# Planned order of an attention and MoE kernel: finer fillers, quartered transposes, ScalarE as a third copier

## The chip, the core and the metric

The kernel runs on one core of one Trainium2 chip. The time is device microseconds of one launch, from the first instruction to the last with what the device adds around them; several runs are taken and the median stands for the kernel. The core has five instruction streams that run by themselves and wait for each other by semaphores: PE (TensorE, matmuls), DVE (VectorE), ACT (ScalarE), POOL (GpSimd) and SP (SyncE). DMA transfers are issued from POOL, SP or ACT and run on 16 shared DMA engines.

## What is computed

Attention over a short window in each of 8 batches and 8 heads, and then a gated two-layer network over the 4608 tokens. Four heads attend to the last 32 positions, four to every fourth of the last 128:

```python
scores = scale * np.matmul(q, k.transpose(0, 1, 3, 2))        # 8 x 8 x 576 x 576, D = 64
mask_plain = (rel >= 0) & (rel < window)                       # window 32
mask_dil = (rel >= 0) & (rel < window * dilation) & (rel % dilation == 0)   # dilation 4
...
attn = attn / (np.sum(attn, axis=-1, keepdims=True) + 1e-09)
return np.matmul(attn, v).astype(np.float32)
```

```python
x = np.ascontiguousarray(attn_out.transpose(0, 2, 1, 3)).reshape(B * S, H * D)   # 4608 x 512
h = x @ w_in                                                   # 512 x 2048
g = h * (1.0 / (1.0 + np.exp(-beta * h)))
return (g @ w_out).astype(np.float32)                          # 2048 x 512
```

## The kernel before

The work comes in nine token tiles of 512 and eight batches of 576 tokens. For each token tile there are 16 up-projection slots (`slot_h`, line 870: four matmuls of 128x128 by 512 columns into one PSUM bank, then a tanh on ACT at line 879 and a gate on DVE at line 884 that writes `g`) and four down-projection blocks (`block_cols`, line 905: 16 matmuls of 512 columns each in four parts, then an evacuation and a store). For each batch there is `attention`: scores, exponentials on ACT (line 602), masks on DVE or POOL (line 606), products with V, and normalising on DVE (lines 621 and 622). The result of a batch goes into `xT`, from which the up-projection of a later token tile reads.

Nothing of the order is written out by hand. Every piece of work is an `Op` with the engines that may run it, each with an estimated duration, with its dependencies, its PSUM banks and a due time. `Plan.run` walks through a simulated clock: for every engine it looks for the operations that can start soonest, takes the one that is due first, and emits its instructions, so each engine's instruction stream is the planner's order. Where an operation names several engines, the planner chooses. `NUDGE` shifts the start that single operations (by their number) are compared with. `CAPS` limits how many PSUM banks of a kind may be open; up-projection slots have three. `free[e]` is the time at which the planner takes engine `e` to be free again. `o.sbuf` marks operations that are kept from running on DVE and POOL at once.

Fillers are matmuls on zeros (line 1018, 256 columns) whose results nobody reads. Until 80 us of planned time the planner puts one where PE would otherwise have nothing to do for over 300 ns, and books 225 ns for it.

The first three batches (`DIRECT = 3`) load K and Q on POOL's DMA queue into `st` (line 390) and turn them on PE: `t_transposes` makes 12 transposes for a dilated half and 18 for a plain one (lines 466 and 473), into one PSUM bank each. A plain transpose takes a piece of 64 rows and 64 columns; of the four 64x64 quarters of the array, the two on the diagonal are used, one for each half of the partitions. The copies out of PSUM (line 239, the helper `copy`) go to `kT`, `qT`, `dk` and `dq` on DVE or ACT. The later batches get these by DMA transposes out of DRAM, issued on SP (line 456).

Three more copies serve attention, all at line 239: `mixed` gathers the last dilated keys into `dkt`, `padded` writes two pieces of `qt`, and `spread` brings V of the dilated heads into `vd` with a column of ones beside it. They may go on DVE or POOL.

Of the kernel before, what the change touches and what calls it, by code (L numbers as in the profile page):

```python
# [9 lines left out]
BF16 = mybir.dt.bfloat16  # L10
ACT = mybir.ActivationFunctionType
ALU = mybir.AluOpType


class Group:
# [21 lines left out]
class Plan:  # L37
# [3 lines left out]

    CAPS = {"h": 3, "p": 4, "o": 2, "z": 4, "a": 8, "s": 5, "w": 6}
    SWITCH = 95
    NUDGE = {4: 150, 6: -150, 14: -900, 49: 150, 117: -400, 126: 150, 135: 400, 182: -150, 184: 900,
        231: 900, 353: 150, 430: -900, 453: -900, 493: -400, 671: 400, 674: -900, 704: 400,
        933: 150, 985: 400, 1015: -150, 1017: -400}
    LAT = {"PE": 210, "ACT": 45, "DVE": 45, "POOL": 60, "SP": 0}
    NEAR = {"PE": 40, "ACT": 60, "DVE": 60, "POOL": 60, "SP": 0}

    def __init__(self, banks):  # L50
# [9 lines left out]
    def run(self, filler=None, filler_until=0.0):  # L60
# [36 lines left out]
        while n_left:  # L97
            best = None
            near = {}
            for o in avail:  # L100
                base = o.ready
                at = {e: max([free[e], base] + [t for x, t in o.group.read.items() if x != e]
                             if o.group is not None and e != "PE" else [free[e], base]) for e, d in o.engs}
                if o.sbuf:
                    at = {e: max(t, port["DVE" if e == "POOL" else "POOL"]) for e, t in at.items()}
                fin = min(at[e] + d for e, d in o.engs)
                for e, d in o.engs:
                    start = at[e]
                    if start + d > fin + 100:
                        continue  # L110
                    if o.dma and len(lanes[e]) >= 8:
                        start = max(start, lanes[e][-8])
                    if o.acquire is not None:
                        start = bank_at(o.acquire, start)
                        if start is None:
                            continue
                    near.setdefault(e, []).append((start, o, d))
            picks = []
            for e, c in near.items():
                first = min(s + o.bias for s, o, _ in c)  # L120
                s, o, d = min((x for x in c if x[0] + x[1].bias <= first + self.NEAR[e]), key=lambda x: (x[1].vt, x[0]))
                picks.append((s, o.vt, e, o, d))
            assert picks, "no work can start"
            s, _, e, o, d = min(picks, key=lambda x: (x[0], x[1]))
            if filler is not None and s <= filler_until and free["PE"] + 300 < s:
                now = free["PE"]
                open_banks = {x.bank for x in held.values()}
                spare = [b for b, t in bank_free.items() if b not in open_banks and t <= now]
                if spare:
                    filler(max(spare, key=lambda b: -bank_free[b]))  # L130
                free["PE"] = now + 225
                halves = False
                continue
            for g in o.acquire or ():
                open_banks = {x.bank for x in held.values()}
                g.bank = min((b for b, t in bank_free.items() if b not in open_banks and t <= s + 1e-6),
                             key=lambda b: -bank_free[b])
                held[id(g)] = g
                g.left = len(g.users)
            o.fn(e)  # L140
            if e == "PE" and o.halves != halves:
                halves = o.halves
                d += self.SWITCH
            free[e] = s + d
            if o.sbuf:
                port[e] = s + d
            o.start, o.end = s, s + d + self.LAT[e]
            if o.group is not None and e != "PE":
                o.group.read[e] = o.end
            if o.dma:  # L150
                at = max(dma_free[e], s + d + 900)
                other = max(dma_free.values()) - at
                dma_free[e] = at + o.dma + max(0.0, min(o.dma, other))
                o.end = dma_free[e] + (o.lat or 1100)
                lanes[e].append(o.end)
            avail.remove(o)
            n_left -= 1
            for x in o.next:
                x.waits -= 1
                x.ready = max(x.ready, o.end)  # L160
                if not x.waits:
                    avail.append(x)
            for g in list(held.values()):
                if o in g.users:
                    g.left -= 1
                    if not g.left:
                        del held[id(g)]
                        g.release = max(u.end for u in g.users)
                        bank_free[g.bank] = g.release
                        ends.append(g)  # L170
            ends[:] = [g for g in ends if g.release > s - 5000]
# [9 lines left out]
def kernel(  # L181
# [10 lines left out]
    nc = tc.nc  # L192
# [41 lines left out]
    def bank(g, dt=FP32):  # L234
        b = BANKS[g.bank][:]
        return b if dt == FP32 else b.bitcast(BF16)
# [221 lines left out]

    def t_transposes(g, z, kind, i):
        if kind == "D":
            tp = bank(g, BF16)[:, 0:S].rearrange("p (s x g) -> p s x g", s=3, x=2)
            for s_ in range(3):
                for x in range(2):
                    nc.tensor.transpose(tp[:, s_, x], std[z][:, x, (2 * s_ + i) * P:(2 * s_ + i + 1) * P],
                                        ident_b[0:2 * GD, 0:2 * GD])
        else:
            tp = bank(g, BF16)[:, 0:S].rearrange("p (j g) -> p j g", j=RP)
            for j in range(RP):  # L470
                for h in range(2):
                    rows = slice(64 * h, 64 * h + 64)
                    nc.tensor.transpose(tp[rows, j], stp[z][rows, i, j * D:(j + 1) * D], ident_b[rows, rows])

    def at_once(x, i, h):

# [8 lines left out]
    def used(key, o):  # L485
        last.setdefault(key, []).append(o)
# [43 lines left out]
    def attention(b, ld, names, vts):  # L530
# [2 lines left out]
        vt_of = dict(zip(names, vts))  # L533
        kv = b % 2
        if b < DIRECT:
            for n in [x for x in names if x[0] in "KQ"]:
                z, kind, i = "KQ".index(n[0]), n[1], int(n[2])
                vt = vt_of[n]
                g = Group("a")
                srcs = ld["qk", z, 0 if kind == "P" else 4]  # L540
                srcs = srcs if isinstance(srcs, list) else [srcs]
                tr = plan.op([("PE", (18 * mm(64) if kind == "P" else 6 * mm(QT)))],
                             lambda e, g=g, z=z, kind=kind, i=i: t_transposes(g, z, kind, i),
                             srcs + [ident], vt, acquire=g)
                used(("st", z), tr)
                turned.append(tr)
                def evac(e, g=g, z=z, kind=kind, i=i):
                    tp = bank(g, BF16)[:, 0:S]
                    if kind == "P":
# [11 lines left out]

        def mixed(e):
            copy(e, dkt[kv], dk[kv][:, :, :, CT - KTL:].rearrange("p r h k -> p h k r"))
        o = plan.op([("DVE", 450), ("POOL", 550)], mixed,
                    (steps["KD0"] + steps["KD1"] if b < DIRECT else ready["D"][0:1]) + war(("dkt", kv)), vt_of["T"] - .01, sbuf=True)
        used(("dk", kv, 0), o)
        used(("dk", kv, 1), o)
# [2 lines left out]
        for c in range(2):  # L570
            def padded(e, c=c):
                rows = slice(64 * c, 64 * c + 64)
                copy(e, qt[kv][rows, c].rearrange("p r h u -> p (r h) u"),
                     dq[kv][rows, :, :, P:].rearrange("p r h u -> p (r h) u"))
            o = plan.op([("DVE", 250), ("POOL", 500)], padded,
                        (steps["QD0"] + steps["QD1"] if b < DIRECT else ready["D"][1:]) + [fill1] + war(("qt", kv)),
                        vt_of["T"] - .01, sbuf=True)
            used(("dq", kv, 0), o)
# [8 lines left out]
        vdeps["P", 0] = [ld["vp"][0], (fill3, fill4)[kv], fill3]  # L587
        def spread(e):
            copy(e, vd[kv][:, :, :, 0:D], vd16_of[b])
        o = plan.op([("POOL", 1100), ("DVE", 620)], spread,  # L590
                    [ld["vd"][0], (fill3, fill4)[kv]] + war(("vd", kv)), vt, sbuf=True)
        used("vd16" if b < DIRECT else ("st", kv), o)
        wrote(("vd", kv))
# [5 lines left out]
        def exp_and_mask(key, sop, g, vt, n, sc, w, m, tiles):  # L599
# [4 lines left out]
            if b >= ADDED or key == ("T",):  # L604
                def mask(e):
                    E[e].tensor_tensor(out=w(), in0=w(), in1=m(), op=ALU.mult)  # L606
                ex = plan.op([("POOL", 170 + 2.2 * n), ("DVE", 160 + .8 * n)], mask,
                             [ex] + [mask_tail if key == ("T",) else mask_ops["D" if key[0] in (2, 3) else "n"]],
                             vt, sbuf=True)
            wrote(*tiles)  # L610
# [16 lines left out]
        for name in [n for n in names if n[0] in "ST"]:  # L627
# [112 lines left out]
            for n, x in enumerate(xs):  # L740
                for h in range(2):
                    exp_and_mask((x, j, h), sop, gs[2 * n + h], vt, 3 * QT,
                                 lambda g=gs[2 * n + h]: bank(g)[:, 0:3 * QT].rearrange("p (a n) -> p a n", a=3),
                                 lambda x=x, j=j, h=h: pt[x][:, 6 * j:6 * j + 6].rearrange(
                                     "p (a h) n -> p h a n", h=2)[:, h, :, 0:QT],
                                 lambda j=j: mask_n[:, 1 + j:4 + j],
                                 [("pt", x, i) for i in range(3 * j, 3 * j + 3)])
        for name in [n for n in names if n[0] in "VU"]:
# [303 lines left out]
```

## Time and profile before

| what | value |
|---|---|
| three runs | 305.56, 305.77, 302.61 us; median 305.56 |
| the profiled execution | 302.53 us, of which the span from first to last instruction is 300.8 |
| PE busy | 293.7 us, 2303 matmuls |
| DVE, ACT, POOL busy | 186.6, 169.2, 90.2 us |
| up-projection matmuls, line 870 | 584 |
| down-projection matmuls, line 905 | 608 |
| plain transposes, line 473 | 216 (three batches) |
| fillers, line 1018 | 26, of which 23 in the first 10 us, the last at 24.5 us |
| w_out, two loads | issued at 19.96 and 26.18 us, 16 us each to landing |
| HBM | 37.76 MB read, 18.87 MB written |

A busy matmul engine isn't one at its peak: matmuls overlap, and the duration of one (379 ns for 512 columns) is longer than its share of a stream. The chain of waits gives the share: four in 0.86 us. A table of groups has, for each source line, engine, operation and shape, the busy time, the mean of one, and what ended the idle time before them. The chain of waits follows the execution back from its last instruction, at each step to what released it.

### The profile page before, as it was taken

What the parts mean: (1) busy time and instruction counts of PE and PEld (TensorE: products, weight loads), DVE (VectorE), ACT (ScalarE), POOL (GpSimd) and SP (SyncE); (2) the same over time, 40 slices, a digit from 0 to 9 for tenths busy, and PEclk for the clock granted to TensorE, in tenths of its full rate; (3) what the DMA queues carried; (4) which work ended last, traced back from release to release, by engine and by line L of the source; (5) the groups of instructions that cost most, each with busy time, mean ns of one, the idle gap of its engine ahead of it and who ended that gap; (6) DMA issues with size and microseconds to landing.
All of it is one profiled execution on the core that took longest, in us unless ns stands there. A gap on an engine that the chain in (4) does not pass through costs nothing.

```text
span 300.8 us, 6004 instructions
## 1 busy us (share of the span) xinstructions
PE 293.7 (98%) x2303; PEld 149.2 (50%) x2303; DVE 186.6 (62%) x421; ACT 169.2 (56%) x304; POOL 90.2 (30%) x131
## 2 busy tenths in 40 slices
PE   8899999999999999999999999999999999999995
PEld 5655546555544444445444544445444444444454
DVE  4768776988958655877567756865871543343300
ACT  3769855767547554765574557454763644555311
POOL 8987574844090105500741092100000000000000
DMA  7999999999799989999999989993142100010122
GB/s 144 184 210 201 207 180 224 164 171 185 180 157 190 155 156 186 166 135 227 178 159 169 225 152 141 173 214 96 37 97 91 37 35 36 35 37 35 58 82 72
DMA packets 111248, 41.98 MB, mean 140 GB/s; under 512 B 87620, under 2 KB 104596, under 8 KB 111220
## 3 DMA queue, kind: packets, MB, share of 16 engines
q0 software_dynamic: 60336, 18.58, 59.2%
q1 hardware_dynamic: 50740, 22.95, 37.2%
q8 instruction: 18, 0.29, 0.4%
q14 instruction: 10, 0.08, 0.1%
q10 hardware_dynamic: 144, 0.07, 0.1%
HBM read 37.76 MB, written 18.87 MB: 188 GB/s over the span
## 4 chain that ended last, share of the span: by engine, by line
PE 82%; DMA 11%; DVE 2%; ACT 1%; issue 1%; POOL 1%; POOLq 0%; ACTq 0%
PE bank L905 40%; PE bank L870 36%; DMA w_out_bf<-in_moe_w_out_dram 5%; DMA vd<-in_v_dram 3%; DMA st<-in_k_dram 2%; PE bank L787 2%; PE bank L666 1%; PE bank L771 1%; PE bank L694 1%; ACT ptd L602 1%; DVE vd L239 1%; PE bank L756 0%; DVE g L884 0%; DVE xdm L622 0%; PE bank L730 0%
## 5 line engine op out<-in xcount | busy, mean ns | idle before, releaser
L905 PE MATMUL bank<-w_out_bf,g 128*128 128x512 bf16 (+2 forms) x608 | 141.2, 368 | 0.2 <-DMA w_out_bf<-in_moe_w_out_dram 0.2
L884 DVE SCALAR_TENSOR_TENSOR g<-tnh,bank 128x512 bf16<-128x512 bf16 x144 | 97.6, 684 | 69.6 <-ACT tnh L879 68.7
L879 ACT ACTIVATE tnh<-bank,beta_half 128x512 bf16<-128x512 f32 x144 | 98.2, 689 | 73.4 <-PE bank L870 69.6
L870 PE MATMUL bank<-xT,w_in_bf 128*128 128x512 bf16 (+1 forms) x584 | 138.8, 376 | 0.1
L870 PEld LDWEIGHTS <-w_in_bf 128*128 128x128 bf16 x584 | 55.1, 98 | 61.7 <-issue 0.2
L905 PEld LDWEIGHTS <-g 128*128 128x128 bf16 x608 | 54.7, 98 | 56.6 <-issue 0.3
L920 ACT ACTIVATE osb<-bank 128x512 f32<-128x512 f32 (+1 forms) x35 | 20.7, 592 | 30.7 <-PE bank L905 30.3
L602 ACT ACTIVATE pt<-bank 128x384 bf16<-128x384 f32 (+1 forms) x54 | 20.7, 470 | 8.3 <-PE bank L694 6.7
L606 DVE TENSOR_TENSOR pt<-pt,mask_n 128x384 bf16<-128x384 bf16 (+1 forms) x39 | 14.4, 387 | 9.0 <-ACT pt L602 8.7
L602 ACT ACTIVATE ptd<-bank 128x512 bf16<-128x512 f32 x32 | 16.7, 606 | 5.0 <-PE bank L666 5.0
L622 DVE TENSOR_TENSOR xsp<-bank,rcp 96x384 bf16<-96x384 f32 x32 | 17.7, 554 | 1.1
L390 POOL DMA_DIRECT2D vp<-in_v_dram x9 | 14.8, 1643 | 0.4 <-PE bank L809 0.4
L621 DVE RECIPROCAL rcp<-bank 128x4 f32<-128x4 f32 (+2 forms) x72 | 12.8, 178 | 2.8 <-PE bank L787 2.2
L622 DVE TENSOR_TENSOR xdm<-bank,rcp 128x256 bf16<-128x256 f32 x32 | 13.6, 424 | 1.1
L390 POOL DMA_DIRECT2D vt<-in_v_dram x16 | 14.1, 979 | 0.3 <-issue 0.3
L606 DVE TENSOR_TENSOR ptd<-ptd,mask_d 128x512 bf16<-128x512 bf16 x26 | 10.7, 424 | 5.0 <-ACT ptd L602 4.0
L390 POOL DMA_DIRECT2D s<-in_q_dram x10 | 13.6, 1360 | 0.0
L984 POOL COPY pace<-xT 1x2 bf16<-1x2 bf16 x4 | 0.7, 176 | 41.6 <-DMA xT<-x 41.6
L787 PEld LDWEIGHTS <-pt 128*128 128x128 bf16 x192 | 9.3, 97 | 5.7 <-issue 0.2
L390 POOL DMA_DIRECT2D s<-in_k_dram x10 | 11.1, 1110 | 1.0 <-issue 0.9
L239 POOL COPY vd<-st 128x1024 bf16<-128x1024 bf16 x5 | 5.4, 1076 | 19.9 <-DMA st<-in_v_dram 19.9
L787 PE MATMUL bank<-vp,pt 128*128 128x65 bf16 x192 | 10.4, 193 | 0.1
(109 smaller groups left out, 177.5 us busy)
## 6 DMA issues: line engine op xcount, KB each, us to landing
out_dram<-osb SPq DMA_DIRECT2D x35, 256.0 KB, 3.1
s<-in_k_dram POOLq DMA_DIRECT2D x10, 288.0 KB, 6.9
s<-in_q_dram POOLq DMA_DIRECT2D x10, 288.0 KB, 9.9
w_out_bf<-in_moe_w_out_dram POOLq DMA_DIRECT2D x2, 1024.0 KB, 16.0
vp<-in_v_dram POOLq DMA_DIRECT2D x7, 288.0 KB, 16.3
st<-in_q_dram POOLq DMA_DIRECT2D x6, 288.0 KB, 12.1
x<-xsp SPq DMA_DIRECT2D x12, 144.0 KB
st<-in_k_dram POOLq DMA_DIRECT2D x5, 288.0 KB, 13.9
```

The lines of the kernel that those rows point to most:

```text
L239: (nc.scalar.copy if e == "ACT" else E[e].tensor_copy)(out=out, in_=in_)
L390: {"POOL": nc.gpsimd, "SP": nc.sync}[queue].dma_start(out=out, in_=in_)
L602: nc.scalar.activation(out=w(), in_=sc(), func=ACT.Exp, scale=SCALE)
L606: E[e].tensor_tensor(out=w(), in0=w(), in1=m(), op=ALU.mult)
L621: nc.vector.reciprocal(out=r, in_=p[..., D])
L622: nc.vector.tensor_tensor(out=dst, in0=p[..., 0:D], in1=r.unsqueeze(len(p.shape) - 1).to_broadcast(list(p.shape[:-1]) + [D]), op=ALU.mult)
L787: nc.tensor.matmul(pv[:, a, h2, :], lhsT=lhs, rhs=vp[kv][:, (2 * x + h2) * NI + 3 * j + a, 0:D + 1], start=True, stop=True)
L870: nc.tensor.matmul(bank(g)[:, a:z], lhsT=w_in_bf[:, kt, fb * P:(fb + 1) * P], rhs=xT[:, kt, xo + a:xo + z], start=(i == 0 and kt == kts[0] ...
L879: nc.scalar.activation(out=th[:, 0:n], in_=bank(g)[:, 0:n], func=ACT.Tanh, scale=beta_half[:, fb:fb + 1])
L884: nc.vector.scalar_tensor_tensor(out=g_t[t % 2][:, fb, c0:c0 + n], in0=th[:, 0:n], scalar=1.0, in1=bank(g)[:, 0:n], op0=ALU.add, op1=ALU.mult)
L905: nc.tensor.matmul(bank(g)[:, lo:hi], lhsT=g_t[t % 2][:, fb, tb * P:(tb + 1) * P], rhs=w_out_bf[:, fb, lo:hi], start=(fb == 0), stop=(fb = ...
L920: nc.scalar.mul(out=ob[:, lo:hi], in_=bank(g)[:, lo:hi], mul=0.5)
```

## The change

- A filler is now put into a hole of more than 170 ns (before: 300) and booked at 115 ns (before: 225), once the planned time is past `COLD = 5500` ns.
- The plain K or Q of a batch is turned in one operation (`t_quarters`) with two PSUM banks instead of two operations with one each. It has the same 36 transposes; each row half goes in turn to the one and to the other column half, so all four quarters of the array take part. Of the second pair of heads, the two heads stand exchanged between the partition halves, in K and Q alike, and one index in the score's evacuation (`h ^ x`) puts them back. The planner books 306 ns for the set.
- `mixed`, `padded` and `spread` may also go to ACT.
- The planner takes ACT to be free 105 ns earlier and DVE 80 ns earlier after an operation of more than 250 ns (`LAP`), and books fewer ns for `mixed` and for masks on DVE.
- `NUDGE` has other entries.

```diff
+COLD = 5500
...
+    LAP = {"PE": 0, "ACT": 105, "DVE": 80, "POOL": 0, "SP": 0}
...
-            if filler is not None and s <= filler_until and free["PE"] + 300 < s:
+            if filler is not None and s <= filler_until and free["PE"] + (300 if free["PE"] < COLD else 170) < s:
...
-                free["PE"] = now + 225
+                free["PE"] = now + (225 if now < COLD else 115)
...
-            free[e] = s + d
+            free[e] = s + d - (self.LAP[e] if d > 250 else 0)
...
-            tp = bank(g, BF16)[:, 0:S].rearrange("p (j g) -> p j g", j=RP)
-            for j in range(RP):
+    def t_quarters(gs, z):
+
+        tps = [bank(g, BF16)[:, 0:S].rearrange("p (j g) -> p j g", j=RP) for g in gs]
+        half = [slice(64 * h, 64 * h + 64) for h in range(2)]
+        for j in range(RP):
+            for x in range(2):
                 for h in range(2):
-                    rows = slice(64 * h, 64 * h + 64)
-                    nc.tensor.transpose(tp[rows, j], stp[z][rows, i, j * D:(j + 1) * D], ident_b[rows, rows])
+                    nc.tensor.transpose(tps[x][half[h ^ x], j], stp[z][half[h], x, j * D:(j + 1) * D],
+                                        ident_b[half[h], half[h]])
...
-                tr = plan.op([("PE", (18 * mm(64) if kind == "P" else 6 * mm(QT)))],
-                             lambda e, g=g, z=z, kind=kind, i=i: t_transposes(g, z, kind, i),
-                             srcs + [ident], vt, acquire=g)
-                used(("st", z), tr)
+                if kind == "P" and i == 0:
+                    gs = [Group("a") for _ in range(2)]
+                    tr = plan.op([("PE", 18 * 17)], lambda e, gs=gs, z=z: t_quarters(gs, z),
+                                 srcs + [ident], vt, acquire=gs)
+                    quarters[z] = gs, tr
+                    used(("st", z), tr)
+                elif kind == "D":
+                    g = Group("a")
+                    tr = plan.op([("PE", 6 * mm(QT))], lambda e, g=g, z=z, i=i: t_transposes(g, z, i),
+                                 srcs + [ident], vt, acquire=g)
+                    used(("st", z), tr)
                 turned.append(tr)
+                if kind == "P":
+                    g, tr = quarters[z][0][i], quarters[z][1]
...
-        o = plan.op([("DVE", 450), ("POOL", 550)], mixed,
+        o = plan.op([("DVE", 360), ("POOL", 550), ("ACT", 500)], mixed,
...
-            o = plan.op([("DVE", 250), ("POOL", 500)], padded,
+            o = plan.op([("DVE", 250), ("POOL", 500), ("ACT", 290)], padded,
...
-        o = plan.op([("POOL", 1100), ("DVE", 620)], spread,
+        o = plan.op([("POOL", 1100), ("DVE", 620), ("ACT", 1030)], spread,
...
-                ex = plan.op([("POOL", 170 + 2.2 * n), ("DVE", 160 + .8 * n)], mask,
+                ex = plan.op([("POOL", 170 + 2.2 * n), ("DVE", 160 + .53 * n)], mask,
...
-                                     "p (a h) n -> p h a n", h=2)[:, h, :, 0:QT],
+                                     "p (a h) n -> p h a n", h=2)[:, h ^ (x if b < DIRECT else 0), :, 0:QT],
```

## The prediction

> **What bounds the kernel now.** I read the page, then busy time by three stretches, then the chain of waits from 9 to 60 us, then who waits for whom, and last the timeline around the operations that the diff names. First the stretches. Columns: stretch and length, then busy us and instructions of PE, weight loads, VectorE (DVE), ScalarE (ACT) and GpSimd (POOL), granted clock, DMA share, GB/s.
>
> ```profile
> 0.00:36.00 36.00, 32.66 (x452) 21.04 (x453) 25.49 (x72) 24.83 (x51) 28.39 (x54) 1.00 1.20 189
> 36.00:60.00 24.00, 23.32 (x268) 12.72 (x268) 18.97 (x43) 15.12 (x33) 15.62 (x21) 1.00 1.47 191
> 60.00:298.00 238.00, 237.75 (x1586) 115.42 (x1584) 142.11 (x308) 129.29 (x222) 46.22 (x58) 1.00 0.89 128
> ```
>
> From 60 us to the end PE idles 0.25 us in 238, while ACT and DVE are busy 54 and 60%. There only less PE work could help; a faster copy or a better order on another engine can't. The first 60 us are different: DMA moves 190 GB/s there. Its busy share in 40 slices of those 60 us, and the chain (start, length, what):
>
> ```profile
> DMA  0599999999999999999999999999999999999799
> ```
>
> ```profile
> 19.96 15.95 DMA w_out_bf<-in_moe_w_out_dram
> 35.91 0.05 issue
> 35.95 1.04 PE bank L905 x4
> ...
> 38.56 0.86 PE bank L870 x4
> ...
> 41.46 0.88 PE bank L870 x4
> ...
> 55.26 1.68 DVE vd L239
> 56.96 0.68 DVE g L884
> 57.64 0.04 issue
> 57.68 0.60 PE bank L666 x15
> ```
>
> The DMA engines are full from 3 to 56 us. w_out lands at 35.9, and PE is there: it waits only 0.05. So time saved before 36 us becomes a longer wait for w_out, unless PE has other work to put there. It has some: the two runs of L870 x4 at 38.56 and 41.46 are the last up-projection slots of the first token tile, left over past 36 (four full-width matmuls take 0.86, so 0.216 each). They, 1.74 us, are what a quicker front can absorb. From 36 on, PE is the bound, and one stall is plain: a DVE copy of vd took 1.68 where the next gate stood behind it.
>
> **Part by part,** against the profiled execution's 302.53 us (span 300.8 and 1.73 around it).
>
> *Transposes of four pieces.* The timeline has, for the plain transposes and for the nearest 64-column matmuls that use the whole array:
>
> ```profile
> 9.28 0.76 PE L473 MATMUL bank<-ident_b,st 64*64 64x64 bf16 x36 [0.97 <-DMA st<-in_k_dram]
> 10.70 0.47 PE L473 MATMUL bank<-ident_b,st 64*64 64x64 bf16 x18
> 11.53 0.28 PE L635 MATMUL bank<-qt,dkt 128*128 128x64 bf16 x4
> ```
>
> 18 more cost 0.29, so 16 ns each; one at a time costs (0.28-0.193)/3 = 29 ns, 0.193 being the mean of one in the table of groups. Two pieces at once have brought 29 to 16, so I carry the ratio on: four bring 16 to 8. The number of transposes stays: 6 sets (K and Q of 3 batches) of 36, each 0.29 shorter. Bounds: nothing (issue is already the limit) to 6 x 0.29 = 1.74. The two sets of batch 2 run at 53 to 57 us on the full PE: 0.58 counts. The four of batches 0 and 1 (1.16) lie before 36 and count only through the leftover slots. The first copy of a set now waits for all 36 instead of its 18: at 8 ns they end together with today's 18, so nothing is lost; at 16 ns the first copy comes 0.29 later, ahead of 36. The Trainium skill, "TensorE: Matmul & The Clock Gate", section "Wait — 56ns, not 53.3ns?", has a floor of about 25 ns between matmul starts, however small they are; it speaks against any gain from a fourth piece. By it an edit of the transposes would bring 0 and the time would be about 1 us above my sum. The 16 ns of this trace are already under that floor, so I go by the row.
>
> *Copies also on ACT* (dkt, qt, vd). No instruction is added or removed; the order decides who runs it. ACT copies 288 columns in 398 ns and 576 in 640 here, 0.84 ns a column, so vd's 1024 cost about 1.02 us on ACT. The timeline shows what that copy costs DVE at worst:
>
> ```profile
> 55.02 1.67 POOL L390 DMA_DIRECT2D s<-in_k_dram  x1
> 55.26 1.77 DVE L239 COPY vd<-vd 128x1024 bf16<-128x1024 bf16 x1 [0.29 <-DMA vd<-in_v_dram]
> 57.68 0.60 PE L666 MATMUL bank<-dq,dk 64*128 64x128 bf16 x15 [0.65 <-DVE g L884]
> ```
>
> The other two vd copies on DVE took 0.43; this one lay beside a POOL DMA issue and held the gate and PE. On ACT that PE idle of 0.65 goes; bounds 0 (copy stays) to -0.65. If it moves, a tanh of 0.69 queued behind it on ACT is 1.02 late, and the two other PSUM banks that up-projection slots may hold cover that. I take -0.5, nearer the row. The small dkt and qt copies (0.2 to 0.55) I put at nothing, hidden under the same banks; uncovered, a qt copy would cost a score its 0.3.
>
> *Shorter holes filled.* A filler has 256 columns, half of 0.216, so 0.11 each. Today there are 26, 23 of them in the first 10 us, and none after 24.6. A lower threshold adds some until 80 us. Where PE truly waits they cost nothing; where it doesn't, 0.11 each. Bounds: 0 to +2.2 (20 of them); I take 4 that hurt, +0.4, near today's 3 after 10 us. The granted clock is 1.00 everywhere, so I give them no gain. The 20 fillers of the first 4.45 us took 0.22 each, twice that, but below COLD the diff leaves threshold and booking as they were.
>
> *Shorter occupancies, cheaper masks, other biases.* These change the order alone. The booking is closer to the trace: four exponentials in 2.06 us are 515 ns each against 606 alone. What it can bring lies in front: PE's room ahead of w_out, up to the leftover 1.74. The transposes free 1.16 there. I take -1.15 for both together, between 0.58 (the share of batch 1 alone, nearest to w_out) and 1.74. On the other side, an order that misjudges a landing could repeat the 0.65 stall some four times, +2.6.
>
> Sum: -0.58 - 0.5 + 0.4 - 1.15 = -1.83, so 300.7 for an execution like the profiled one. The three runs stand at 302.61, 305.56 and 305.77: two levels, 3 us apart, the profiled one on the lower. I can't tell which the new median will show, so I carry the middle, 304.1, less 1.8: **302.3**; on the lower level it is 300.7, on the upper 303.8.
>
> **The rivals.** *w_out comes earlier.* The biases reorder POOL's queue. A K or Q load is 288 KB, 1.4 us at about 200 GB/s; four of batch 1 are issued ahead of w_out. If three go behind it, the down-projection starts 4.3 us sooner, and 298 comes out. For it: PE waits for that landing. Against: due times in the loads' code are unchanged, and batch 1's own work before 36 would then be missing.
>
> *ACT stands before a landing (slower).* POOL's waits for the copies now allowed on ACT:
>
> ```profile
> POOL vd L239 <- DMA st<-in_v_dram: 19.9, 5, 7.1
> POOL dkt L239 <- DMA dk<-s: 9.8, 4, 3.3
> ```
>
> Columns: total, times, longest. POOL has nothing else to do; ACT has every tanh queued behind. PE can go on for two more slots and the two down-projection parts between them, 4 x 0.86 = 3.45. The two longest waits for vd are 7.05 (before 97.9) and 5.66 (before 187.0): with the copy, 7.05+5.66+2x1.02-2x3.45 = 7.9 us lost, 310 in all. It decides once ACT takes up a vd copy over 2.4 us before its landing. For it: the order is fixed by planned landings. Against: DVE already takes such copies with waits of at most 0.5 for vd.
>
> *Fillers in dense stretches:* it takes 28 that hurt to lose 1%: 306 to 309. *The four pieces don't overlap:* 0.58 and half of 1.16 are missing, 303.5.
>
> **How the numbers follow.** Chances: forecast 0.47, w_out earlier 0.25, ACT blocked 0.14, fillers 0.06, no overlap 0.08. Within 1% (302.5 to 308.6) is about what a measurement can tell from no change, the runs themselves spreading 1%. The forecast straddles that border, half on each side; w_out earlier is nearly all faster; a third of no overlap is: 0.225+0.225+0.025, 0.47. Slower: most of ACT blocked, half of the fillers, a little of the forecast's +2.6 end on the upper level, 0.17. The rest, 0.36, is same. The range runs from 297.5 (w_out earlier on the lower level) to 308.5 (the upper level with +2.6 and some fillers); outside lie ACT blocked and scraps. The forecast's own range is 300 to 305.
>
> **What would show it.** Right: plain transposes x36 in about 0.48 instead of 0.76; L870 leftovers after w_out gone or halved; no PE wait on a gate behind vd near 56 us; PE as dense after 60 us; w_out landing within 0.5 us of 35.9. Wrong: w_out landing before 34; ACT waiting for st<-in_v_dram for microseconds with PE idle after; fillers between 40 and 80 us beside a PE that was full.

## The result, and the profile after

The changed kernel took 305.26 us (median of 20 runs, 303.32 to 307.88), the kernel before 303.19 (20 runs, 302.27 to 309.26): a ratio of 1.0054, 95% interval 1.0034 to 1.0075. It is half a per cent slower. The profile that came with the result, 307.88 us, had a stretch at a lower granted clock; the lines below are from another profile of the same kernel, 305.26 us with a span of 303.5, against 302.53 and 300.8 before.

First the stretches of the changed kernel, columns as before: length, busy us and instructions of PE, weight loads, DVE, ACT and POOL, granted clock, DMA share, GB/s.

```profile
0.00:36.00 36.00, 34.02 (x459) 21.11 (x459) 26.01 (x69) 27.13 (x56) 27.33 (x53) 1.00 1.21 191
36.00:60.00 24.00, 23.38 (x279) 13.07 (x279) 19.11 (x45) 10.79 (x26) 11.20 (x16) 1.00 1.26 166
60.00:298.00 238.00, 236.89 (x1567) 113.19 (x1566) 144.73 (x315) 130.12 (x224) 45.95 (x55) 1.00 0.93 128
```

PE looks busier before 36 us (34.02 for 32.66), but see what it was busy with. The same stretches for the fillers alone, and for the up-projection alone, of the changed kernel (PE busy and count, weight loads, clock, DMA):

```profile
0.00:36.00 36.00, 8.07 (x44) 4.82 (x44) 1.00 1.21 191
36.00:60.00 24.00, 2.52 (x17) 1.49 (x17) 1.00 1.26 166
```

```profile
0.00:36.00 36.00, 14.89 (x72) 6.59 (x72) 1.00 1.21 191
36.00:60.00 24.00, 5.46 (x24) 2.11 (x24) 1.00 1.26 166
```

Fillers are 61 instead of 26, and 17 of them stand between 36 and 60 us, where there was none. The up-projection has 72 matmuls before 36 us and 24 behind; before the change it was 64 and 32. So two slots did move ahead of w_out. Busy time hides what that is worth, so I add up, over neighbouring matmuls, the time from one start to the next less what the columns of the first one need (512 columns 216 ns, fewer in proportion, at least 27 ns, and half of that for a matmul of 64 rows; where the next one starts sooner, the difference counts as negative), and call it idle. It is an estimate from the starts of the two traces:

| stretch | idle before | idle after | fillers before | fillers after |
|---|---|---|---|---|
| to 36 us | 9.98 | 6.75 | 26 | 44 |
| 36 to 60 us | 2.87 | 2.23 | 0 | 17 |
| from 60 us | 3.63 | 6.47 | 0 | 0 |

A filler is worth 0.109 us. Up to 60 us, idle and fillers together are 15.7 us before (9.98+2.87+26x0.109) and 15.6 after (6.75+2.23+61x0.109). The front gained nothing, although its transposes became cheaper (216 of them by 8 ns, 1.7 us; since both columns count a transpose at 13.5 ns, this saving stands in the idle column). The span grew by 2.7 us, and the idle time behind 60 us by 2.8: the loss lies behind 60 us, where the prediction's sum had no term.

The chain of waits of the changed kernel around 40 us shows what stands where the two slots were (start, length, what):

```profile
36.39 1.32 ACT pt L620 x4
37.73 1.59 DVE pt L624 x2
39.32 0.34 DVE vd L244
39.66 1.19 DVE g L902 x2
40.85 0.71 DVE pt L624 x2
41.68 0.42 DVE xdm L640
42.23 0.43 DVE xdm L640
42.70 0.40 PE bank L842 x4
```

Before the change PE stood in the chain here without a gap until 42.3 us, with the L870 runs at 38.56 and 41.46 among the pieces. Now it runs through DVE: masks, a vd copy, gates, masks, norms. With their up-projection slots gone ahead, PE's own timeline has this at the same place:

```profile
41.67 0.49 PE L1036 MATMUL bank<-zero 128*128 128x256 bf16 x3
42.70 0.38 PE L842 MATMUL bank<-ident_b,xdm 128*128 128x128 bf16 x4 [0.54 <-DVE xdm L640]
42.92 0.82 PE L1036 MATMUL bank<-zero 128*128 128x256 bf16 x6
```

The leftover slots were not left over: they were what PE did while DVE worked on batch 1. On DVE, masks took 2.89 us (6 of them) between 36 and 60 us, before 0.97 (4); POOL had 2.07 (3) for 3.90 (5).

Around 56 us, the place of the old stall, in the changed kernel:

```profile
55.97 0.48 PE L480 MATMUL bank<-ident_b,st 64*64 64x64 bf16 x36
56.37 0.18 POOL L1002 COPY pace<-g 1x2 bf16<-1x2 bf16 x1 [7.40 <-DVE g L902]
57.34 0.48 PE L480 MATMUL bank<-ident_b,st 64*64 64x64 bf16 x36
57.48 0.42 DVE L244 COPY vd<-vd 128x1024 bf16<-128x1024 bf16 x1
57.60 1.67 POOL L395 DMA_DIRECT2D s<-in_k_dram  x1
```

The sets of 36 take 0.48, the vd copy 0.42, and PE doesn't stop. But the second line matters more than I saw. `pace` (line 984 before the change, line 1002 after it) is a tiny POOL copy that reads the first gate of token tile 1, and batch 3's eight loads stand behind it on POOL. Before the change:

```profile
53.77 0.17 POOL L984 COPY pace<-g 1x2 bf16<-1x2 bf16 x1 [4.95 <-DVE g L884]
```

The first gate of tile 1 comes 2.6 us later, and so do the loads. The DMA row of the page shows a hole for it, in the eighth slice (53 to 61 us), and the rate falls from 164 to 86 GB/s there; first before, then after:

```profile
DMA  7999999999799989999999989993142100010122
GB/s 144 184 210 201 207 180 224 164 171 185 180 157 190 155 156 186 166 135 227 178 159 169 225 152 141 173 214 96 37 97 91 37 35 36 35 37 35 58 82 72
```

```profile
DMA  7999999699979999999799989994133000100122
GB/s 166 178 209 201 206 178 225 86 156 169 209 174 181 156 135 221 152 157 252 128 184 137 193 152 178 177 200 125 37 92 97 35 35 36 37 35 35 50 90 69
```

And SP's queue has a new order around 84 us. DMA issues of `x<-xdm` store batch 3's dilated rows. `xT<-x` are batch 2's two back-transposes, the DMA transposes that bring its result rows into `xT`. Before, then after:

```profile
76.86 3.61 SPq L526 DMA_TRANSPOSE xT<-x  x2
81.76 0.33 SPq L925 DMA_DIRECT2D out_dram<-osb  x1
82.14 1.79 SPq L507 DMA_DIRECT2D x<-xdm  x2
```

```profile
80.68 1.46 SPq L534 DMA_TRANSPOSE xT<-x  x1
82.97 0.94 SPq L515 DMA_DIRECT2D x<-xdm  x1
84.02 1.31 SPq L534 DMA_TRANSPOSE xT<-x  x1
```

The second back-transpose is issued behind a store that waits for batch 3's norms, at 84.0, where both had been issued between 76.9 and 80.5. The loads of batch 4 wait for that transpose: their `pace` comes at 87.83 instead of 82.61. The Trainium skill, "DMA: Bandwidth & Descriptors", section "Anatomy of one DMA — SWDGE (gpsimd) path", says that DMA engines never wait for semaphores and that any wait is held by the sequencer that issues; it fits these rows, where a waiting store holds up the transpose behind it. Over the run `pace` waits 50.9 us for `xT<-x` instead of 41.6. At 115.8 PE stands before an up-projection that needs batch 3's rows:

```profile
115.84 3.61 PE L888 MATMUL bank<-xT,w_in_bf 128*128 128x512 bf16 x16 [0.71 <-ACT osb L938]
```

The line names ACT as the releaser, but batch 3's transpose landed at 115.70, just ahead of this start, and the `pace` copy that waits for it ran at 115.85; by the starts, PE lost 0.875 there. Most of the rest of the 2.8 us is another 0.49 at 162.6 and 1.0 spread over 60 to 100 us (idle 2.26 there instead of 1.21).

### The profile page after: what moved, and what is told of

It is laid out like the page before. It is cut to its first block, busy times and chain, and to the rows that moved or that the text cites. A ratio compares the mean times of both kernels' runs of the same rounds, so it can differ in the third digit from the quotient of the medians.

```text
span 306.1 us, 6067 instructions
## 1 busy us (share of the span) xinstructions
PE 297.0 (97%) x2338; PEld 150.2 (49%) x2338; DVE 190.8 (62%) x429; ACT 169.1 (55%) x306; POOL 83.9 (27%) x121
## 4 chain that ended last, share of the span: by engine, by line
PE 83%; DMA 8%; DVE 4%; POOL 2%; ACT 1%; issue 1%; ACTq 0%; DVEq 0%; POOLq 0%
PE bank L923 38%; PE bank L888 36%; DMA vp<-in_v_dram 6%; DMA st<-in_q_dram 2%; PE bank L805 2%; DVE pt L624 1%; PE bank L1036 1%; PE bank L789 1%; PE bank L712 1%; POOL s L395 1%; DVE xdm L640 1%; PE bank L684 1%; PE bank L470 1%; PE bank L774 1%; DVE g L902 1%
## 5 line engine op out<-in xcount | busy, mean ns | idle before, releaser
L888 PE MATMUL bank<-xT,w_in_bf 128*128 128x512 bf16 (+2 forms) x584 | 138.7, 376 | 0.0
L923 PEld LDWEIGHTS <-g 128*128 128x128 bf16 x608 | 55.4, 98 | 57.4 <-issue 1.0
L938 ACT ACTIVATE osb<-bank 128x512 f32<-128x512 f32 (+1 forms) x30 | 17.2, 576 | 28.2 <-PE bank L923 28.1
L624 DVE TENSOR_TENSOR pt<-pt,mask_n 128x384 bf16<-128x384 bf16 (+1 forms) x42 | 16.4, 415 | 5.4 <-ACT pt L620 5.1
L940 DVE TENSOR_SCALAR osb<-bank 128x512 f32<-128x512 f32 (+1 forms) x8 | 5.3, 658 | 14.8 <-PE bank L923 14.7
L395 POOL DMA_DIRECT2D s<-in_q_dram x10 | 13.5, 1349 | 0.0
L1036 PE MATMUL bank<-zero 128*128 128x256 bf16 x61 | 10.1, 303 | 1.1 <-DVE warm L303 1.1
```

The costliest lines, as they stand in the source:

```text
L395: {"POOL": nc.gpsimd, "SP": nc.sync}[queue].dma_start(out=out, in_=in_)
L888: nc.tensor.matmul(bank(g)[:, a:z], lhsT=w_in_bf[:, kt, fb * P:(fb + 1) * P], rhs=xT[:, kt, xo + a:xo + z], start=(i == 0 and kt == kts[0] ...
L923: nc.tensor.matmul(bank(g)[:, lo:hi], lhsT=g_t[t % 2][:, fb, tb * P:(tb + 1) * P], rhs=w_out_bf[:, fb, lo:hi], start=(fb == 0), stop=(fb = ...
L938: nc.scalar.mul(out=ob[:, lo:hi], in_=bank(g)[:, lo:hi], mul=0.5)
L1036: nc.tensor.matmul(BANKS[b][:, 0:256], lhsT=zero[:, 0:P], rhs=zero[:], start=True, stop=True)
```

## The experiments

Theories: the fillers hurt where PE is full (A); the order within the new code hurts, namely the late release of batch 3's loads and the SP order that follows (B); the transposes in quarters cost something elsewhere (C). Four runs on one chip, the kernel before at 302.65.

**The changed kernel again.**

> The changed kernel as it is, for a profile at full clock. In its first profile vp of batch 3 landed at 80.3 us (74.4 before), PE stood still 2.1 us ahead of batch 3's products with V, and the clock fell to 0.83 from 80 to 90 us. Late-loads theory (the pace copy that releases batch 3's loads ran at 56.4 us instead of 53.8): the late landing is there at full clock too, PE stands still 1 to 3 us near 79 us, ratio to the kernel before 1.004 to 1.008. Filler theory (61 fillers against 26, 0.11 us each): no stall of PE over 0.5 us after 60 us, and still the same ratio. Chance theory (the first profile was a disturbed run): the ratio is within 0.2% of 1.

305.12, ratio 1.0087 (1.0053 to 1.012). The loss is there again; its profile is the one above. But the stop of 1 to 3 us near 79 that the late-loads theory asked for is missing: batch 3's V rows landed at 78.3, and PE ran on. The largest stops from 36 us on are 0.71 at 41.9 and 0.875 at 114.8, where the filler theory had none above 0.5 after 60 us. Neither theory fits here as it was put.

**No fillers past 5.5 us**, the order unchanged.

```diff
-                if spare:
+                if spare and now < COLD:
```

> The changed kernel in exactly its order, but the fillers past 5.5 us of planned time (44 of 61) are not emitted; they were only matmuls on zeros. Filler theory: 1.5 to 3.8 us faster than the changed kernel, ratio 0.993 to 1.000. Late-loads theory: the fillers stand in front of landings that PE waits for anyway; within 0.5 us of the changed kernel, ratio 1.004 to 1.008, and PE idle between 36 and 46 us grows by about 1.6 us.

306.71, 1.012 (1.0084 to 1.0156). Not faster, and above what either theory said. 44 fillers are gone (4.8 us), and to 60 us 3.7 us of idle time stand in their place (6.75 to 9.55 and 2.23 to 3.16). So nearly four fifths stood in holes, and the hole at batch 1's norms is now plain: PE stops for 0.97 us at 40.8 and 0.88 at 42.2. The other 1.1 us came to nothing behind 60 us, where PE stopped for 2.27 us at 77.8, ahead of products with V whose masks stand behind a copy that waited for batch 3's V rows (landed at 79.2). A falls.

**Batch 3's loads released early.**

```diff
-   xT[0:1, 0, mid - 1:mid + 1] if b - 2 >= BY_DMA else g_t[b % 2][0:1, 0, 0:2]))
+   xT[0:1, 0, mid - 1:mid + 1] if b - 2 >= BY_DMA else zero[0:1, 0:2]))
```

> The changed kernel in exactly its order, but the two values that POOL copies to pace batch 3's loads come from the tile of zeros instead of the first gate of token tile 1, so the loads are issued as soon as POOL reaches them, about 49 us instead of 56.5. Late-loads theory: no gap in the DMA between 52 and 57 us, vp of batch 3 lands before 76 us, the stall near 79 us is gone, 1.5 to 2.5 us faster than the changed kernel, ratio 0.997 to 1.001. Filler theory: the same as the changed kernel, 1.004 to 1.008. A third way: the early loads delay batch 2's landings, and it is slower, 1.01.

305.98, 1.0108 (1.0059 to 1.0157). The V rows of batch 3 landed at 71.8 instead of 78 to 80; PE didn't stop near 79, as it hadn't in the changed kernel's own profile; but it stopped for 2.39 us at 113.3. SP issued nothing from 77.6 to 82.6, because the second back-transpose stood behind the store that waits for batch 3's norms. An early release alone brings nothing with this SP order.

**Transposes in halves again**, the rest unchanged (the index in the score's evacuation goes back with them).

```diff
-        for j in range(RP):
-            for x in range(2):
+        for x in range(2):
+            for j in range(RP):
...
-                    nc.tensor.transpose(tps[x][half[h ^ x], j], stp[z][half[h], x, j * D:(j + 1) * D],
+                    nc.tensor.transpose(tps[x][half[h], j], stp[z][half[h], x, j * D:(j + 1) * D],
```

> The changed kernel in its order with the plain transposes in the old pattern, two pieces at once (same 36 a set, same two banks). If four at once do save 0.29 us a set: 0.3 to 1 us slower than the changed kernel (batch 2's two sets run while PE is the bound), a set of 36 takes 0.75 again, ratio 1.006 to 1.009. If PE waits for landings in all three batches: within 0.2 us, ratio as the changed kernel's.

306.57, 1.011 (1.0076 to 1.0145), beside 1.0087 with quarters. The timeline of both, quarters first:

```profile
9.24 0.48 PE L480 MATMUL bank<-ident_b,st 64*64 64x64 bf16 x36
```

```profile
9.20 0.75 PE L480 MATMUL bank<-ident_b,st 64*64 64x64 bf16 x36
```

The quarters do what they should, 0.27 a set, and the median is 1.45 lower with them; the intervals overlap. C falls.

**The SP order, and the order of batch 4's V load**, on another chip (before: 304.35). A small addition moves operations in the emitted order and leaves the plan as it is: the store behind the back-transpose, batch 4's dilated V load ahead of another V load on POOL, both, and both with the early release.

```diff
+COLD, AHEAD, BEHIND, MOVED = 5500, {668: [667]}, {445: [583]}, [583, 667]
...
-            o.fn(e)
+            for f in [self.ops[n].fn for n in AHEAD.get(o.n, ())] + [o.fn] * (o.n not in MOVED) + [self.ops[n].fn for n in BEHIND.get(o.n, ())]: f(e)
```

> The changed kernel with one instruction moved on SP: the second back-transpose of batch 2 (x to xT) stands ahead of the store of batch 3's dilated rows (xdm to x), as it does in the kernel before; every other stream is the same. Queue theory (SP's stream is in order, so the transpose waits behind a store whose data is not ready): the second transpose issues 1.3 us earlier than the 84.0 us of the changed kernel, or up to 5 us earlier where loads are early; the pace copy of batch 4 runs before 87 us, and the ratio to the kernel before falls by 0.002 to 0.006, to 1.003 to 1.007. Rival (batch 2's attention itself ends late, in PE's and DVE's order): the store's data is ready at that time anyway, and the ratio stays at 1.008 to 1.011.

> The changed kernel with one instruction moved on POOL: the 256 KB load of batch 4's dilated V is issued third to last before its two tail pieces, the last K/Q cast and the plain V, as in the kernel before, not behind them. Queue theory: its landing goes from 112.5 to about 104 us, the copy and the products with V of batch 4 no longer hold PE at 113 to 116 us, 0.5 to 1.2 us faster than the changed kernel, ratio 1.004 to 1.007. Rival (at that place PE waits for the back-transpose of batch 3 into xT, the next thing to be late): the stall at 115 us stays, ratio 1.008 to 1.011.

> Both moves, on SP and on POOL, in the changed kernel. Queue theory: the two stalls are what the change lost after 60 us, so 1 to 2.5 us faster than the changed kernel, ratio 1.000 to 1.005. Rival: stalls only change places, ratio 1.007 to 1.011.

> Both moves and the pace copy of batch 3 that reads zeros and so releases the loads as soon as POOL gets there (about 49 us). Queue theory: the DMA has no gap from 2 to 100 us, batch 3's and batch 4's loads land 5 us earlier than in the changed kernel, PE has no stall over 0.5 us after 60 us; what the front gained stays, and the kernel is as fast as the one before or up to 1% faster, ratio 0.990 to 1.000. Rival (landings don't matter after 60 us, the order on PE and DVE does): as the changed kernel, 1.007 to 1.011.

| run | us | ratio to before | 95% interval |
|---|---|---|---|
| store behind the transpose | 304.83 | 1.0039 | 1.0003 to 1.0076 |
| V load ahead | 305.86 | 1.0066 | 1.0035 to 1.0096 |
| both moves | 305.25 | 1.0034 | 1.0000 to 1.0069 |
| both, early release | 304.26 | 1.0020 | 0.9996 to 1.0044 |

With the store moved, the two transposes are issued together again, the stop near 115 is gone, and idle time from 60 us is 4.95 instead of 6.47. SP's queue in that run:

```profile
79.61 3.63 SPq L534 DMA_TRANSPOSE xT<-x  x2
83.30 0.93 SPq L515 DMA_DIRECT2D x<-xdm  x1
```

Batch 4's `pace` comes at 86.23 there, 1.6 earlier than in the changed kernel; the other 3.6 of the 5.2 us remain. The V load's place alone brings nothing that shows: its load lands at 101.9 instead of 112.5, but the other V load now lands at 113.9 instead of 111.1, and PE stops for 1.49 us at 113.5. With the early release on top of both moves, `pace` comes at 48.9, 81.8 and 110.9, all earlier than before the change (53.8, 82.6, 115.6), and the kernel can't be told from the one before; it isn't faster, though its expectation went down to 0.990.

The changed kernel itself didn't run on this chip. The nearest to it is the run with the V load ahead, which has the late release and the SP order of the changed kernel; its 12 runs took 305.22 to 307.03, and the 12 with both moves and the early release 303.35 to 304.63. The two don't overlap: the SP order and the early release together take away 1.6 us (305.86 to 304.26), the SP order alone about 1.0 (305.86 to 304.83). That is the plainest evidence of the cause in the changed kernel. Against the changed kernel's own intervals on other chips the last row is less clear: it ends at 1.0044, theirs begin at 1.0034 (the result), 1.0053 and 1.0061.

**From the other side: parts of it in the kernel before**, and the changed kernel without its new biases (third set, before: 303.46).

The first was meant to try the SP order in the kernel before.

```diff
+ALU = mybir.AluOpType; AHEAD, BEHIND, MOVED = {451: [589]}, {}, [589]
```

> The reverse test: the kernel before with one instruction moved on SP, the store of batch 3's dilated rows (xdm to x, second half) ahead of the second back-transpose of batch 2, as the changed kernel has it; every other stream is the kernel before's. Queue theory: the transpose issues at about 83 us instead of 79, the pace copy of batch 4 runs at 87 us instead of 82.6, and the kernel is 1 to 2 us slower than the one before, ratio 1.003 to 1.007. Rival (PE has other work in this order): the pace is late, and the ratio stays within 0.998 to 1.002.

307.43, 1.0158 (1.0128 to 1.0189). It tried something else: the store now came ahead of batch 3's norms in the program, so it stored rows that were there before (that part of batch 3's dilated result is left old), and the norms had to wait for the store. PE stopped for 3.3 us at 81.6. It says nothing on the theory; the order is put into the kernel before rightly further down.

**The quarters alone**, the old biases kept on their operations; the edit is the `t_quarters` part of the diff.

> The kernel before with the quartered plain transposes alone (two sets a batch, booked at 306 ns; numbers of the biases kept on their operations). The planner's order changes a little with the booking. Size by the prediction's sum: 0.58 us faster from batch 2's sets, up to 1.7 if the front can use the rest: ratio 0.994 to 0.998. Landing theory (PE ends up waiting for w_out and V whatever it saves ahead): between 0.996 and 1.000. Worse than 1.003 would say that the order's other places decide more than the part itself.

303.9, 1.0032 (1.0009 to 1.0054). Even the part that saves 0.27 a set makes the kernel slower, by a third of a per cent. The planner, with one operation booked at 306 ns for a set in place of two, gives another order, in which the release comes at 54.27 (before 53.77) and batch 4's at 85.73 (82.61); that these are what costs isn't shown.

**The changed kernel without biases.**

```diff
-    NUDGE = {4: 900, 12: 900, 97: 400, 99: 150, 165: -900, 173: 150, 241: 60, 247: 400, 250: 900,
...
+    NUDGE = {}
```

> The changed kernel with an empty table of biases; the rest of the change stays. The order is the planner's own, and in it too one store of batch 3 (first half) stands ahead of batch 2's second back-transpose. If the new biases are what costs: faster than the changed kernel, ratio 0.998 to 1.003. If the bookings and the cheaper masks cost, with any biases: 1.005 to 1.012.

305.93, 1.0089 (1.0047 to 1.0132). The new biases aren't needed for the loss. What the rest of the change makes without them has both marks again: the release at 55.73, and on SP a store between the two transposes.

```profile
79.98 1.39 SPq L531 DMA_TRANSPOSE xT<-x  x1
82.67 0.88 SPq L512 DMA_DIRECT2D x<-xdm  x1
83.65 1.37 SPq L531 DMA_TRANSPOSE xT<-x  x1
```

**All mends together**: both moves, the early release, no late fillers.

> The kernel with both moves and the early pace, without the 44 fillers past 5.5 us of planned time. Without them the changed kernel met batch 3's late landing at 78 us; here that landing is early. Landing theory: PE waits ahead of 46 us for what the fillers covered, and the ratio stays at 1.000 to 1.004. Filler theory: the fillers' 4.8 us were in the way, and 1 to 3 us come back: 0.990 to 0.998.

303.48, 1.0006 (0.998 to 1.0031): not to be told from the kernel before, nor, by the intervals, from the run with the fillers (1.0020). No gain came out of the change in any run.

**The late order put into the kernel before.** Here `pace` and batch 3's loads, and the second back-transpose, are to be made late in the old kernel (fourth set, before: 303.39; the last two on another chip, before: 302.7).

The changed kernel beside them, without an edit:

> The changed kernel as it is, for a ratio on the same chip as the three that follow: 1.005 to 1.009.

```diff
+ALU = mybir.AluOpType; AHEAD, BEHIND, MOVED = {}, {589: [451]}, [451]
```

> The kernel before with one instruction moved on SP: the second back-transpose of batch 2 stands behind both stores of batch 3's dilated rows. Queue theory: it issues at 84 us instead of 79, the pace copy of batch 4 runs at 87 us instead of 82.6, and the kernel is 0.5 to 2 us slower, ratio 1.002 to 1.006. Rival (only the order on PE, DVE and ACT counts): 0.998 to 1.001.

```diff
-   xT[0:1, 0, mid - 1:mid + 1] if b - 2 >= BY_DMA else g_t[b % 2][0:1, 0, 0:2]))
+   xT[0:1, 0, mid - 1:mid + 1] if b - 2 >= BY_DMA else g_t[b % 2][0:1, 2, 0:2]))
```

> The kernel before with the pace copy of batch 3 reading a gate two slots later (third slot of token tile 1 instead of the first), so the loads of batch 3 are issued 3 to 4 us later, at 57 to 58 us; no stream changes its order. Late-loads theory: a gap in the DMA at 55 to 58 us, vp of batch 3 lands at 77 to 79 us instead of 74.4, ratio 1.002 to 1.006. Rival: PE has enough other work, 0.998 to 1.001.

Both edits together:

> The kernel before with both: the late pace of batch 3 and the late back-transpose of batch 2. If the two are the cause of the changed kernel's loss, the kernel before now has its ratio, 1.004 to 1.009, with PE stalls of 0.5 us and more between 75 and 120 us. If not, 0.998 to 1.002.

The gate that `pace` now reads is emitted behind it, so there was nothing to wait for: it ran at 49.0, early, not late. Both runs with it so tried the early release in the old kernel, and that is no gift: PE stops near 58 to 60 us (three times 0.5 to 0.9). The first of these stops waits for a `qt` copy on DVE that took 2.47 us, from 56.39 to 58.86, where such a copy takes 0.18; POOL's issue of batch 3's V load, now early, ended at 58.84. A true delay needs `pace` and the first loads behind the gate of the second slot in the program:

```diff
+ALU = mybir.AluOpType; AHEAD, BEHIND, MOVED = {}, {301: [524, 525, 527], 589: [451]}, [451, 524, 525, 527]
...
+   xT[0:1, 0, mid - 1:mid + 1] if b - 2 >= BY_DMA else g_t[b % 2][0:1, 1, 0:2]))
```

That is the last run; the one ahead of it has the release alone, without the entry 589.

> The kernel before, in which the release of batch 3's loads waits for the gate of the second slot of token tile 1 instead of the first, so it comes at about 57 us instead of 53.8 (the changed kernel has it at 56.4). If the late release makes the changed kernel's loss behind 60 us, this is 1.004 to 1.009 of the kernel before, vp of batch 3 lands at 77 to 80 instead of 74.3, and PE stops for 0.5 us or more near 78. If the late release costs only where SP's order is changed too, or not at all, it is 0.998 to 1.003.

> The kernel before with the late release of the run before and with batch 2's second back-transpose issued on SP behind the store of batch 3's rows, as in the changed kernel. If these two together make the changed kernel's loss behind 60 us, this is 1.006 to 1.012 of the kernel before, with PE stops near 79 and near 114. If the loss comes from the front (36 to 56 us) itself or from other orders, it is below 1.004.

| run | us | ratio to before | 95% interval |
|---|---|---|---|
| changed kernel beside them | 305.81 | 1.0095 | 1.0061 to 1.0128 |
| late transpose | 303.61 | 1.0017 | 0.9997 to 1.0036 |
| early release | 304.09 | 1.0047 | 1.0022 to 1.0071 |
| early release, late transpose | 304.95 | 1.0063 | 1.0040 to 1.0087 |
| late release | 304.49 | 1.0030 | 0.9993 to 1.0066 |
| late release, late transpose | 304.33 | 1.0041 | 1.0013 to 1.0069 |

In the last two `pace` came at 56.05 and 55.85, as in the changed kernel, and batch 4's at 87.00 and 88.04. Neither delay alone can be told from nothing; the two together make the old kernel 0.4% slower. The expectation for that was 1.006 to 1.012, with stops near 79 and 114, or below 1.004; it fell between, and the stops were elsewhere: the largest, 1.37 us at 140.2, stands ahead of products with V whose masks follow a copy that waited for a later batch's V rows (landed at 140.65, before the change 137.51). The run with the late transpose alone stops for 1.57 us at the same place.

The changed kernel was 1.0054, 1.0087 and 1.0095 in its three measurements. In it, the SP order and the late release make most of the loss, since with both taken away (and the V load moved) none is left that can be measured. In the old kernel the same two delays cost 0.4%, by the interval anything from 0.1 to 0.7. That is weaker evidence: the early release cost the old kernel as much (1.0047), and the quarters alone not much less (1.0032). So another reading stays: that the old order loses some tenths of a per cent to changes of many kinds. No run tries it with changes that leave the loads alone. How the rest divides between the other changes of order after 60 us stays open, as does each delay's own share.

## Why the prediction was wrong

The time itself, 305.26, lies in the range, but the forecast was 1.8 us gained, and 1.6 to 2.9 were lost (0.54% of 303.19 to 0.95% of 303.39).

- **The base.** I took the three runs for two levels and started from 304.1. Of 20 runs of the kernel before 16 stand between 302.27 and 304.31; their median is 303.19. They don't show two levels 3 us apart, and two of the three runs that I had were high ones. This was worth 0.9 in the forecast's place, and nothing in its sign.
- **Transposes, -0.58 on the path.** Right as a mechanism: 0.48 for 0.76, 8 ns each. Here the Trainium skill's floor of about 25 ns between matmul starts ("TensorE: Matmul & The Clock Gate", section "Wait — 56ns, not 53.3ns?") doesn't hold for four 64x64 pieces, as the 16 ns of two had foretold. But alone it gave 1.0032: the time was lost again in the planner's new order, by which step isn't shown.
- **The vd copy, -0.5.** The stall went, not by ACT: no vd copy went there (POOL has four, DVE four); ACT took dkt and qt copies, which I had put at nothing.
- **Fillers, +0.4.** 35 more came. By the run without them at most 1.1 us of the 44 late ones was in the way, so the term was somewhat small; it isn't what decided, since taking them away didn't make the kernel faster.
- **The order, -1.15: the step that failed.** "What a quicker front can absorb" was wrong. The two slots did move ahead of w_out, and a hole opened where they had been, since PE has to wait for DVE's work on batch 1 there; up to 60 us idle time and fillers are 15.6 us for 15.7. So the front, where all four terms of the sum lie, gained 0.1 us in all instead of 1.83, and nothing of the 1.15 is left. I had looked at what PE did at 38 and 41 us and not at what it was waiting for underneath. A slot in a chain can be cover for another engine. (No run puts the two slots alone back behind w_out.)
- **From 60 us on, put at nothing.** The sum had no term there, on the ground that PE idled 0.25 us in 238. That is by busy time, in which matmuls overlap; by the starts it was 3.6 us, and the change made it 6.5.
- **The other side, "+2.6, four times the 0.65 stall"**, had the right size by luck and the wrong mechanism. What the runs point to isn't a landing that the order misjudged at a copy, but two release points: the POOL copy that lets batch 3's loads go, and an SP queue in which a store with a wait stands ahead of a transpose. I never followed the queues of SP and POOL behind the operations that move, and wrote that from 60 us "a better order on another engine can't" help: true, but a worse one can hurt.
- **The rivals.** w_out's halves landed at 35.67 and 42.11 (before 35.91 and 42.31): not earlier. ACT waits for no landing of V; those waits are still POOL's:

```profile
POOL vd L244 <- DMA st<-in_v_dram: 14.6, 3, 7.8
POOL dkt L244 <- DMA dk<-s: 9.6, 2, 7.3
```

## What to carry to other kernels

Before work is moved ahead in a planned order, ask what it covers where it stands: leftover work in a stretch that waits for another engine is not slack. Where transfers are released by a tiny operation that reads a result, find that operation and its source first, and the queue behind it; a change of order that moves the source by 2.6 us moved eight loads with it. And when bookings change, compare each DMA queue's order before and after, since one waiting store ahead of a transpose cost about 1 us here, against 1.7 that the cheaper transposes saved.

## What the runs showed beyond that

- Four 64x64 transposes at once start every 8 ns ((0.48-0.195)/35), two at once every 16.
- The vd copy of 128x1024 on DVE took 0.42 beside POOL's DMA issues at 57.5 us, and 1.77 before the change, so an issue beside it isn't enough. But the long copies do end with an issue: that of 1.77 us at 57.03, 0.35 behind POOL's at 56.68; a `qt` copy (usually 0.18) of 2.47 us in the early release at 58.86, the issue at 58.84; one of 1.02 in the run with both moves and the early release at 61.36, the issue at 61.34. What decides which copy is held isn't shown.
- A stop of PE doesn't always cost clock. After 2.3 and 2.4 us without work (the run without late fillers and the early release) the granted clock stayed at 1.00; after 3.3 us, in the run with the store ahead of the norms, it was 0.66 for 5 us:

```profile
80.00:85.00 5.00, 1.98 (x20) 0.98 (x19) 0.89 (x4) 0.60 (x1) 0.00 (x0) 1.00 0.73 153
85.00:90.00 5.00, 4.74 (x35) 2.10 (x36) 2.15 (x9) 1.12 (x3) 3.93 (x7) 0.66 0.58 100
```

The Trainium skill, "TensorE: Matmul & The Clock Gate", section "What's actually happening", has the clock halved after one idle window of about 3.4 us that runs freely. The two shorter stops fit it. The longer one, 3.3 us, lowered the clock though it doesn't fill such a window, and the profile that came with the result has a clock of 0.73 from 80 to 85 us after a stop of only 2.25 us; there the measurement decides. The traces do show windows: in every one of them that has clock records, the changes of clock stand whole multiples of 3.41 us apart, and each low stretch within the span lasts 3.41 us at half. So what counts, as an estimate from the starts, is how much of one window PE was idle. The 2.25 us fell into the window from 78.92 to 82.33, idle for 67%, and the 3.3 us into one idle for 91%; both were followed by a low stretch. Of the windows after 10 us that none followed, the most idle was at 60%. The 2.39 us of the early release were cut in two by a border at 114.98, into windows idle for 44 and 33%, and the clock stayed.
